# Attention values as 64-row products in two row groups and two banks

## The chip, the cores and the metric

The kernel runs on one core of a Trainium2 chip. The metric is device microseconds of one execution of the whole program, the median of several runs. Three runs of the kernel before gave 2386.85, 2388.28 and 2392.48 us.

## What is computed

One transformer block on 2048 rows of width 576: a modulated layer norm, attention with 32 heads of 18 columns, a residual, a second modulated layer norm, a SiLU feed-forward of width 4608 and a second residual. All arrays are float32.

```python
def _A_ref(x, wqkv, wo):                       # H = 32, Dh = 18
    qkv = (x @ wqkv).reshape(B, S, 3, H, Dh)   # then q, k, v by head
    scores = jnp.einsum("bhqd,bhkd->bhqk", q, k) * (Dh ** -0.5)
    p = _softmax(scores, axis=-1)
    o = jnp.einsum("bhqk,bhkd->bhqd", p, v)
    return o_rows @ wo
def _B_ref(x, w1, w2):
    return _silu(x @ w1) @ w2
h = _layernorm(x) * (1 + ca) + sa
x = x + ga * _A_ref(h, A_wqkv, A_wo)
h = _layernorm(x) * (1 + cb) + sb
x = x + gb * _B_ref(h, B_w1, B_w2)
```

The change touches the einsum that gives `o`, the product of the attention weights and the values.

## The kernel before

The attention runs over four blocks of 512 query rows and, in each block, over eight groups of four heads: 32 groups. A group has 64 score products for its row maxima (`slot_mm`, L896, tile `psa`; VectorE reduces each in L898) and 64 for the weights themselves (`slot_b`, L979, tile `psb`; ScalarE takes the exponential into `pt` in L981). A *slot* is one product of each kind: a `psa` of a later group (38 pairs ahead, `LEAD`) on one half of the array's rows and a `psb` of the present group on the other half, side by side. Everything that contracts over few rows is cut this way, into products of 64 rows whose two halves of the array work at the same time; the code calls this the mode "half".

The values of a group (`pv`, L983) are accumulated over 16 key tiles of 128 rows. For one key tile, four products of 128 rows by 32 columns stand side by side in four column groups, one per head, and write four strips of one bank, `psv` (18 columns of values, one column of ones for the softmax's denominator, padding). One such step of four heads is the unit in which values are scheduled. After the last step ScalarE copies the bank to `ov` (L961), four transposes turn it (`out_b`, L996, `pso`) and VectorE divides by the denominators (L1004, L1007). Products with the full 128 rows and 128 columns, mostly transposes, are a third mode, "full".

Between slots and values TensorE works on *fill*: pieces of the projections in the first block (`psqk`) and afterwards the output projection (`psp`) and the feed-forward (`ps`) of the block before. Fill products are 64-row pairs too (class `Pair`, L652): in the first half of a piece's steps rows 0 to 63 write the first bank and rows 64 to 127 the second, in the second half the other way round, so that each pair of pieces needs two banks at once. ScalarE and VectorE read them out (L1300, L1302, and L1172, L1175 for the residual sums). The last block's own feed-forward has no attention left beside it; it runs at the end in full mode (L646).

The order of TensorE's work is a text, `ORDER`: `s` is a slot, `f` the next piece of fill, a digit that many steps of values, `x` the transposes for maxima or outputs. A class `Sim` reads it and, from a table of durations and a model of the queues, decides where the other engines' instructions are issued; its `rings` say how many banks each use has. The work before the first values is ordered in the same manner by a class `Start`. In total there are 2048 slots and 512 steps of values. The steps stand in 311 unbroken runs of digits.

PSUM has eight banks. Up to the point where the feed-forward begins, `psF` (fill) has two, `psA` (first score products and transposes) three, `psB` (second score products) two and `psV` (values) one. After it, `psF` has three and `psA` two.

Of the kernel before, what the change touches and what calls it, by code (L numbers as in the profile page):

```python
# [73 lines left out]
    "ssffsfsffsfsfssfsfsfsfsfsfsfs11ss1ss1sfsfsfsfsfsfsfssfsfsfssfsfsffss2ss1ss1ss1ss1ssfsfsfssfsfss1ss1xss1ss1sfssfssfssfsfs"  # L74
    "sfsfssfssfss1ssfss1ssfxss11ss1ss1ss1ss1ssfsfssfssfssfssfssfsfss1ss1ss1ss1ss1ss1ss1xss1ssfssfssfssfss11ssfsfssfsfsfssfssf"
    "sxss11ss1ss1ss1ss1ssfsfssfsfsfsfsfs11ssfsfsfsfsfsfssfssfsfsfssfs1ss1ss1xss1ss1ss1ss1ss1ssfsfssfsfs1fssfssfsfsfsxss2ss1ss"
    "1ssfssfsfssfsfsfsfssfssfsfssfsf1ss1ssffss1ss1ss1ss1ss1ss1xss1ssffsfssfssfssfsfsfsfssfssfs1ss1ssffss11fss1ss1ssfssfsxss11"
    "ssffssffss1ss1ss1ssfssfsfsfssfssfssfssfss1ss1ss1xss1ss1ssf1fss1ssfssfsfssfssfsfsxss11ss1ss1sfssfsfsfssfssfssfssfsfss1fss"
    "1ss1ss1ss1ss1ssfssfssfsfssfssfss1xss1ss1ss1ss1ss1sfssfssfssfssfssfssfsxss2ss1ss1ss1ss1ss1ssfss1ssssfsfsfssfssfssfssfssfs"
    "s1ss1ss1xss1ss1ss1ss1ss1ssfssssssfssfsssxss11ss1ss1ss1ssssssfssfssssfss1sssssss1ss1ss1ss1ss1ss1ss1xssssss1ss1ss1sssx1ssf"  # L80
    "ssffss1sff1sfsffsfsfssssf11fssffffsfffssfffffffssffffsffsfs1fffsffffssfffsffffssfffsffffsffsfffffss13fssfsffss1fsfsfsfsf"
    "sfsffssfffsffsffs3xsfsfsfsfsfsffssffsfsfsfsfsfs2sfsfffsfsffssffsfsfsfsfsfs1xsf3ssffssss1ss11fssffsffssffsffssffsfsfs1sfs"
    "fsffssffsfsfs1sfsfsffssffsffss13xsfsfsfsfsfffssffsfsfsfsfsfs12sfsfffssfffssffsfsfsfsffss1sffsx2fss1ss1sss1fssffsffss1fss"
    "fffssfffssf11fsfsffssffsffssffsffssffsff1sffssffsfsffssfffsffsfsfs13xsfsfsfsfsfsfsfssfsfsfsfsfsffss2fssf1fss1ss1xs1fssff"
    "sffss1sfsfsffssffsffss1sfsfsffssffsfsfs12ssffsffssffsfsfs1sffsfsfsfsffssfffssffsfsfs22xsfsfsfsfsfsfsfssfsfsfsfsfsfsfs2fs"
    "sf1ss1ss1ss1ssffsfsfsffsxffffssffsffss1sfsfsffssffsffss2ssffsffssffsffss3sfsfsfsfsfsffssffsfsfsfffss13xsfsfsfsfsfsfsfssf"
    "sfsfsfsffss1ss1ssf1ssffxsf11fssffsffss1sfsfsffssffsfsfs1sfsfsffssffsfsfs2sfsfsffssffsfsfs31ssffsfsfsfsffssfffsfsfsfsfs11"
    "xsfsffsfsfsffss1ss1ss1ssffsfsfsfsfs1ss1ssf11ffffssffffsxffffssffsfsfs1ssffsffssffsffss1sfsfsffssffsffss21sfsfsfsfsfsffss"
    "ffsfsfsfsffss2ss2xfsfsfsfsfsfsfssfsfsfsfsfsfs1ss1ss1sfs111ffffssffsffssffsffssffffsxffffssffffssffsffssffffs2sfffsfsfffs"
    "sffsfsffssffs121fssfffsfsffssffsfsffsfsfs1fsfs1fss1ss1ss1xsfssffsffssffsffssffsfsfs1sfsfsffssffsfsf1fsfsffssffsffss3fsfs"  # L90
    "ffssfffssfffffsffxs12ss1ssfssfs1ssfss1ssfssfs1ss1ssfsfsss1ss1sfsxfssffffssfffsffffssfffffffssffffssffff11fffffffssffffff"
    "fssffffssffffss1ffssfffffssfffffffs112sffffsfffssfffffffssffffsffffsfff1ffx1fsfsfsfsfsffssffsfsfsfsffss111sfsffsfsfsffss"
    "ffsfsfsfsfsfs1sfsffffsffssfffssffsff3xsfsfsffssffsfsfs21sfsfsffssffsffsxffffssffsffss11ssffffssfffsfs2ssffsfsfsfsffssffs"
    "fsfsfsfsfs21ssfffsfsfsffssffsfsfsfsffss22ssffsffssffsffss2xsfsfsffssffsfsfs11sfsfsffssffsffss1fsfsffssffsfsfs111xffsfsff"
    "ffssffsfsfsfsfsfs11ssffffsfsffssffsfsfsfsfsfs211sfsfsffssfffsfs1ssffsffssffsffss2ssffffssffsfsfs11xsfsfsffssffsffss11sfs"
    "fsfsfsfsffssffsffsfsfsfs3xffsfsfsfsffssffsfsfsfsfsfs12ssffffssffsfsfs1ssffsffssffsffss2ssffsffssffffss1sfsfsffssffffss22"
    "xsfsfsfsfsfffssffsfsfsfsffs2sfffsfsfsffssffsfsfsfsfsfs21xffffssffsfsfs1sfsfsffssffsffss11ssffsffssffffss2ssffsffssffsfsf"
    "2ssffsfsfsfsffssffsfsfsfffss112xsfsfsfsfsfsffssfffssffsfsfs2ffffssffsfsfs11ssffsffssffsfsfs11xffffssfffsfs1sfsfsffssffsf"
    "fss1sfsfsffssfffssffsfsfsfsffss22ssffsfsfsfsffssffsfsfsfsffss12xsffsffssffsfsfs21ssffsffssffsffsxffffssffsfsfs1fsfsffssf"
    "fsffss111sfsfsffssfffssffsfsfsfsffss22ssffsfsfsfsffssffsfsfsfsfsfs3sfsfffssffsffssffsffssffsffs2xsfsfsffssffsfsfs1sfsfsf"  # L100
    "fssffsfsfs2sfsfsfsfsfsffssffsffsfffx3ss1fffssf11fssffffssffsfsfs1ssfffffffssfffsfffsfs2sfsfffssfffsfs1sfffsffffssffffsff"
    "fssffffssffffss11xsfsfffsfffssfffsfsffsfs31fsfsffsfffssfffsffsffs1sffffssffffsfffssffx11fsfsfsfsfffssffsfsfsfsfsfs21ssff"
    "fsfsfsffssffsfsfsfsffss3fsfsfsffsffssffsfsfsfsfsfs11sffffssfffssf1xsfsfsffssffsfsfs22sfsfsffssffsffsxffffssffsfsfs21sfsf"
    "sfsfsfsffssffsfsfsfsffss3ssfffsfsfsffssffsfsfsfsfsfs1fsfffssfffsfs1ssffsffssffsffss2ssffffssffffss112xsfsfsffssffsffss2f"
    "ssffsfsfsffssffsfsfsfsfsfs3xffsfsfsfsffssffsfsfsfsfsfs12sffsffssffsfsfs1sfsfsffssffsfsfs1ssffsffssffsffss2sfsfffssfffssf"
    "211xsfsfsfsfsfsffssffsfsfsfsfsfs11sffsfsffsffssfffsfsfsfsfs13xffsffssffsfsfs1sfsfsffssffsffss11ssffsffssffsfsfs11ssffsff"
    "ssffsffss2sfsfsfsffsffssffffssfffss21xsfsffsfsfsffssffsfsfsfsfsfs11sffffssfffssf2xffffssffsffss11fsfsffssffsfsfs1sfsfsff"
    "ssfffsfs2fssffsfsfsffssffsfsfsfsfsfs22sfsfsfsfsfsffssffsfsfsfsfsfs111xsfsfffssffsffss11ssffsffssffsffsxffffssffsfsfs12ss"
    "ffsffssfffssf11sfsfsfsfsfsffssffsfsfsfsfsfs111ssfffsfsfsffssffsffssffsfs111ssffffssffffs1sfsfffssffsfsfs2xsfsfsffssffsff"
    "ss11sfsfsffssffsfsfs11xsfsfsfsfsfffssfffsfsfsfsfs111sfsffssffsffssffsfsfsfsffss111sffsffssffsfsfs1ssffsffssffsfsfs12ssff"  # L110
    "sffssffsfsfs1fssfffssffsffs21ffx"
# [34 lines left out]
class Sim:  # L146


    def __init__(self, fill, ends, loads):
# [6 lines left out]
        self.rings = {"f": [0] * 2, "a": [0] * 3, "b": [0] * 2, "v": [0]}  # L156
# [230 lines left out]
    def values(self, n):  # L387
# [187 lines left out]
def tile_adaln_block(ctx: ExitStack, tc: tile.TileContext, x, wqkv, wo, w1, w2, c, wfirst, wcol, out):  # L575
# [1273 lines left out]
```

## Time and profile before

| what | us |
|---|---|
| median of three runs | 2388.28 |
| profiled execution | 2393.49 |
| its span, first to last instruction | 2391.7 |
| TensorE busy | 2336.2 |
| VectorE busy | 1782.0 |
| ScalarE busy | 1487.1 |
| GpSimd busy | 584.7 |
| first and last start of a value product | 171.1 and 2110.8 |

The span is from the first to the last instruction; the time of the execution has a little around it. In the profile PE is TensorE, PEld its weight loads, DVE VectorE, ACT ScalarE, POOL GpSimd and SP the queue that issues the transfers. Timeline rows give the start, the duration until the last of the merged instructions ends, the engine, the line, and what is written from what. Matmuls overlap and their ends are modelled, so distances between starts say more than durations. A float32 product appears as two records, since it takes two passes; the score and fill products are of a form that takes one. The granted TensorE clock is 0.998 over the span.

### The profile page before, as it was taken

Reading aid. Unit: us, or ns where it says so; the run is one execution under the profiler, and the core shown is the slowest. Engines: PE = TensorE matmul, PEld = TensorE weight load, DVE = VectorE, ACT = ScalarE, POOL = GpSimd, SP = SyncE. Lnnn points to the kernel's source line nnn. Section 1 sums busy time; section 2 is a strip of 40 time slices with the busy share of each in tenths; the row PEclk is TensorE's granted clock in tenths of the full one; section 3 lists DMA queues with packets and bytes.
Section 4 is the critical chain, followed back from the end, with each engine's and each line's share of the span. In section 5 each row is a group of like instructions: output and inputs, shape, how many; then the busy total and the mean of one; then the engine's idle time right before and its main releaser. Section 6 shows DMA issues by size and latency. Waiting matters only on the chain.

```text
span 2391.7 us, 52731 instructions
## 1 busy us (share of the span) xinstructions
PE 2336.2 (98%) x20528; PEld 1635.2 (68%) x20528; DVE 1782.0 (75%) x3179; ACT 1487.1 (62%) x2711; POOL 584.7 (24%) x729
## 2 busy tenths in 40 slices
PE   5999999999999999999999999999999999999999
PEld 4885545545666666676767777777677777688998
DVE  7878888888877887877777877788878878234333
ACT  4237777776766777766577766776767777722121
POOL 4203233314544334443211111111211111110000
PEclk9999999999999999999999999999999999999999
DMA  7758787756555555555555445454545554435663
GB/s 244 254 187 266 252 255 240 260 173 201 200 182 172 173 191 182 171 191 190 172 183 175 149 157 176 166 181 164 186 157 172 186 191 159 138 122 216 209 206 115
DMA packets 210296, 452.29 MB, mean 189 GB/s; under 512 B 22594, under 2 KB 78306, under 8 KB 210050
## 3 DMA queue, kind: packets, MB, share of 16 engines
q1 hardware_dynamic: 210050, 448.93, 56.7%
q8 instruction: 164, 2.69, 0.5%
q14 instruction: 82, 0.67, 0.1%
HBM read 362.51 MB, written 85.80 MB: 187 GB/s over the span
## 4 chain that ended last, share of the span: by engine, by line
PE 88%; DVE 5%; DMA 3%; POOL 2%; issue 2%; ACT 1%; SPq 0%; ACTq 0%; POOLq 0%; DVEq 0%
PE ps L652 27%; PE psv L989 18%; PE psa L896 13%; PE psb L979 10%; PE ps L646 10%; PE psqk L652 4%; DVE mx L898 2%; PE psv L652 1%; PE psp L652 1%; PE pso L996 1%; DMA raw<-in_w 1%; PE psp L646 1%; DMA kt<-kscr 0%; POOL raw L1069 0%; POOL w2t L1075 0%
## 5 line engine op out<-in xcount | busy, mean ns | idle before, releaser
L898 DVE TENSOR_REDUCE mx<-psa 128x1 f32<-128x512 f32 x2048 | 1343.6, 686 | 288.3 <-PE psb L979 149.6
L981 ACT ACTIVATE pt<-psb 128x512 f32<-128x512 f32 x2048 | 1164.0, 597 | 498.3 <-PE psb L979 293.3
L979 PE MATMUL psb<-qt,kt 56*128 56x512 f32 x2048 | 803.2, 426 | 4.6 <-ACT pt L981 2.4
L896 PE MATMUL psa<-kt,qt 54*128 54x512 f32 x2048 | 753.5, 414 | 8.7 <-DVE mx L898 5.2
L896 PEld LDWEIGHTS psa<-kt,qt 54*128 54x128 f32 x2048 | 358.2, 185 | 258.3 <-DVE mx L898 141.3
L989 PE MATMUL psv<-pt,vt 128*32 128x512 f32 x4096 | 505.1, 601 | 0.0
L652 PE MATMUL ps<-w2t,g 64*128 64x288 f32 x4992 | 423.5, 294 | 3.2 <-POOL w2t L1075 1.6
L652 PEld LDWEIGHTS ps<-w2t,g 64*128 64x128 f32 x4992 | 390.1, 185 | 43.1 <-issue 12.7
L979 PEld LDWEIGHTS psb<-qt,kt 56*128 56x128 f32 x2048 | 363.1, 184 | 44.2 <-ACT pt L981 28.8
L652 PE MATMUL ps<-hh,w1t 64*128 64x512 f32 x2160 | 379.0, 393 | 0.1
L1317 POOL TENSOR_TENSOR g<-etmp,g 128x512 fp32r<-128x512 f32 x108 | 137.8, 1296 | 452.2 <-ACT g L1313 406.9
L989 PEld LDWEIGHTS psv<-pt,vt 128*32 128x32 f32 x4096 | 102.4, 109 | 213.0 <-issue 205.6
L652 PEld LDWEIGHTS ps<-hh,w1t 64*128 64x128 f32 x2160 | 216.0, 186 | 40.2 <-issue 4.7
L1179 POOL TENSOR_TENSOR x<-x,gt 128x288 f32<-128x288 f32 x116 | 93.4, 805 | 543.6 <-ACT gt L1175 537.3
L652 PE MATMUL ps<-hl,w1t 64*128 64x512 f32 x864 | 177.9, 391 | 0.0
L1172 DVE TENSOR_TENSOR x<-ps,x 128x288 f32<-128x288 f32 x184 | 83.7, 455 | 116.2 <-PE ps L646 70.7
L646 PE MATMUL ps<-w2t,g 128*128 128x288 f32 x960 | 130.4, 296 | 1.7 <-ACT g L1313 0.9
L646 PEld LDWEIGHTS ps<-w2t,g 128*128 128x128 f32 x960 | 128.6, 188 | 3.3 <-ACT g L1313 1.2
L1306 ACT ACTIVATE eq<-ps 128x512 f32<-128x512 f32 x36 | 21.5, 598 | 146.4 <-PE ps L646 146.4
L646 PE MATMUL ps<-hh,w1t 128*128 128x512 f32 x360 | 106.9, 390 | 0.5 <-DVE hh L626 0.5
L652 PEld LDWEIGHTS ps<-hl,w1t 64*128 64x128 f32 x864 | 88.4, 186 | 13.9
L1025 POOL CAST w1out<-w1raw 128x320 fp32r<-128x320 f32 x72 | 32.4, 450 | 215.0 <-DMA w1raw<-in_w 189.7
(136 smaller groups left out, 2142.2 us busy)
## 6 DMA issues: line engine op xcount, KB each, us to landing
kt<-kscr SPq DMA_DIRECT2D x1024, 108.0 KB
w1t<-w1s SPq DMA_DIRECT2D x144, 640.0 KB
w2t<-w2s SPq DMA_DIRECT2D x108, 576.0 KB
w1s<-w1out SPq DMA_DIRECT2D x72, 320.0 KB
w2s<-w2t SPq DMA_DIRECT2D x36, 576.0 KB
vt<-vscr SPq DMA_DIRECT2D x32, 608.0 KB
qt<-qscr SPq DMA_DIRECT2D x128, 108.0 KB
w1raw<-in_w SPq DMA_DIRECT2D x72, 160.0 KB
```

The lines of the kernel that those rows point to most:

```text
L646: mm(self.ps[late], lhsT=lhsT, rhs=rhs, start=(i == 0), stop=(i == self.n - 1))
L652: done = mm(self.ps[g], lhsT=lhsT[rows], rhs=rhs[rows], start=(s == 0), stop=(s == 2 * self.n - 1))
L896: mm(ps, lhsT=t["q"][64 * j:64 * j + 54, hp, stt * P:(stt + 1) * P], rhs=t["k", kc, hp][64 * j:64 * j + 54, :], start=True, stop=True)
L898: return lambda: nc.vector.tensor_reduce(t["mx"][:, 2 * j + hp, stt, kc:kc + 1], ps, axis=AX.X, op=ALU.max)
L979: mm(ps, lhsT=t["kb", kt // 4, hp][64 * e:64 * e + 56, kt % 4 * P:(kt % 4 + 1) * P], rhs=t["q"][64 * e:64 * e + 56, hp, :], start=True, st ...
L981: return lambda: nc.scalar.activation(t["P"][kt, hp][:, e, :], ps, AF.Exp, scale=SCALE)
L989: mm(t["ps"][32 * h:32 * h + 32, :], lhsT=t["v"][:, c0:c0 + 32], rhs=t["P"][kt, h // 2][:, h % 2, :], start=(kt == 0), stop=(kt == NKT - 1 ...
L996: nc.tensor.transpose(ps[:, s4, :], ov[:, s4 * P:(s4 + 1) * P], ident)
L1025: nc.gpsimd.tensor_copy(d["out"][:, 1], d["raw"])
L1172: nc.vector.tensor_add(c["x1", j][:, hs], ps, c["x1", j][:, hs])
L1179: nc.gpsimd.tensor_add(c["x1", j][:, HH:], c["x1", j][:, HH:], box.pop("gt"))
L1317: (nc.vector if last else nc.gpsimd).tensor_tensor(gt[:, 1, :], d["t"], f(gt[:, 0, :]), op=ALU.subtract)
```

## The change

Each value product of 128 rows is split into two of 64 rows. Rows 0 to 63 of the key tile go to the bank `v0` and rows 64 to 127 to the bank `v1`; each bank has the four heads' strips. After the last step ScalarE copies the first bank into `ov`, and one VectorE addition per group of heads adds the second bank to it (`tensor_add`, 128x512). Values now have two banks, `psF` has two banks throughout, and `psA` two throughout. The planners' rings say the same, and the table of durations stays as it was. The order text is new: 318 runs of digits instead of 311, and 1938 pieces of fill instead of 1952 before the end, where the remaining ones are then issued.

```diff
 ORDER = (
-    "ssffsfsffsfsfssfsfsfsfsfsfsfs11ss1ss1sfsfsfsfsfsfsfssfsfsfssfsfsffss2ss1ss1ss1ss1ssfsfsfssfsfss1ss1xss1ss1sfssfssfssfsfs"
...
+    "ssffsfsfsfsfsfssfsfsfssfsfssfssfss1ss1ssffss1ss1ss1ss1ss1ss1ss1ssfsfsfssfsfssfssfsfssfsfsfsfs2xsfsfsfsfsfsfsfs1ss1ss1ssf"
...
-        self.rings = {"f": [0] * 2, "a": [0] * 3, "b": [0] * 2, "v": [0]}
+        self.rings = {"f": [0] * 2, "a": [0] * 2, "b": [0] * 2, "v": [0]}
...
-        self.rings.update(f=[at[0]] * 3, a=[at[1]] * 2)
+        self.rings.update(f=[at[0]] * 2, a=[at[1]] * 2)
...
         if k0 + n == NKT:
-            self.push((Op(ACT_, 600, self.real and self.real.ov(i), (("p", ("v", i), 0), ("k", ("ov", i)))),), 0, self.t + 200)
+            e = self.real.ov(i) if self.real else (None, None)
+            self.push((Op(ACT_, 600, e[0]), Op(DVE_, 690, e[1], (("p", ("v", i), 0), ("k", ("ov", i))))), 0, self.t + 200)
...
-    psA = ps0.enter_context(tc.tile_pool(name="psA1", bufs=3, space=PSUM))
+    psA = ps0.enter_context(tc.tile_pool(name="psA1", bufs=2, space=PSUM))
...
                 t["ov"] = att.tile([P, QB], F32, name="ov", bufs=1)
-                nc.scalar.activation(t["ov"], t["ps"], AF.Copy)
-
-            return copy
+                nc.scalar.activation(t["ov"], t["ps"][0], AF.Copy)
+
+            return copy, lambda: nc.vector.tensor_add(t["ov"], t["ps"][1], t["ov"])
...
-            t["ps"] = psV.tile([P, QB], F32, tag="v", name="psv2")
+            t["ps"] = [psV.tile([P, QB], F32, tag=f"v{g}", name="psv2") for g in range(2)]
         for kt in range(k0, k0 + n):
             for h in range(4):
                 c0 = kt * VQ + VW * h
-                mm(t["ps"][32 * h:32 * h + 32, :], lhsT=t["v"][:, c0:c0 + 32], rhs=t["P"][kt, h // 2][:, h % 2, :],
-                   start=(kt == 0), stop=(kt == NKT - 1), tile_position=(0, 32 * h))
+                for g in range(2):
+                    rows = slice(64 * g, 64 * g + 64)
+                    mm(t["ps"][g][32 * h:32 * h + 32, :], lhsT=t["v"][rows, c0:c0 + 32], rhs=t["P"][kt, h // 2][rows, h % 2, :],
+                       start=(kt == 0), stop=(kt == NKT - 1), tile_position=(64 * g, 32 * h))
...
-        psF = ctx.enter_context(tc.tile_pool(name="psF2", bufs=3, space=PSUM))
+        psF = ctx.enter_context(tc.tile_pool(name="psF2", bufs=2, space=PSUM))
```

The ring of the `Start` planner for `psA` goes from three to two as well, and its products that borrowed the value bank now take `v0`.

Three places show what stands where. The first is TensorE at one step of values in the first group, between two slots; `pt` are the attention weights of a key tile and two heads, `vt` the values, and the numbers are those of the buffers. Before:

```order
L979 MATMUL psb_2551<-qt_619,kt2_79 128x512
L989 MATMUL psv2_2276<-pt2_2085,vt0_2093 32x512 x2
L989 MATMUL psv2_2276<-pt3_2086,vt0_2093 32x512 x2
L896 MATMUL psa_2565<-kt4_81,qt_1486 128x512
L979 MATMUL psb_2567<-qt_619,kt3_80 128x512
```

After:

```order
L980 MATMUL psb_2395<-qt_619,kt6_83 128x512
L992 MATMUL psv2_2316<-pt4_2087,vt0_2093 32x512
L992 MATMUL psv2_2317<-pt4_2087,vt0_2093 32x512
L992 MATMUL psv2_2316<-pt4_2087,vt0_2093 32x512
L992 MATMUL psv2_2317<-pt4_2087,vt0_2093 32x512
L992 MATMUL psv2_2316<-pt5_2088,vt0_2093 32x512
L992 MATMUL psv2_2317<-pt5_2088,vt0_2093 32x512
L992 MATMUL psv2_2316<-pt5_2088,vt0_2093 32x512
L992 MATMUL psv2_2317<-pt5_2088,vt0_2093 32x512
L897 MATMUL psa_2411<-kt0_77,qt_1450 128x512
```

Four products into one bank are now eight that alternate between two; the four rows of one `pt` are two heads in two halves.

The second is VectorE around the end of the first group's values, where `psa` are first score products and `psqk` a projection. Before, the reciprocal and the first divisions of the transposed output stand between the reductions, and nothing there reads the value bank:

```order
L898 TENSOR_REDUCE mx_2316<-psa_2983 128x1
L898 TENSOR_REDUCE mx_2316<-psa_2987 128x1
L898 TENSOR_REDUCE mx_2316<-psa_3004 128x1
L898 TENSOR_REDUCE mx_2316<-psa_3010 128x1
L1004 RECIPROCAL rec_3040<-pso_3022 128x16
L1007 TENSOR_TENSOR ot_3027<-pso_3022,rec_3040 128x72
L898 TENSOR_REDUCE mx_2316<-psa_3036 128x1
```

After:

```order
L899 TENSOR_REDUCE mx_2300<-psa_3010 128x1
L726 TENSOR_TENSOR qkhl_3030<-psqk_2776,qkhl_3030 128x512
L726 TENSOR_TENSOR qkhl_3033<-psqk_2777,qkhl_3033 128x512
L899 TENSOR_REDUCE mx_2300<-psa_3038 128x1
L964 TENSOR_TENSOR ov_3042<-psv2_2317,ov_3042 128x512
L899 TENSOR_REDUCE mx_2300<-psa_3054 128x1
L899 TENSOR_REDUCE mx_2300<-psa_3069 128x1
```

The addition stands between two reductions.

The third is TensorE between two groups of heads, here the seventh and the eighth: the last value products of the one and what follows. Before, these rows and 32 more come ahead of the next group's first value product:

```order
L989 MATMUL psv2_6552<-pt3_2086,vt0_2093 32x512 x2
L896 MATMUL psa_7018<-kt1_78,qt_6522 128x512
L979 MATMUL psb_7020<-qt_5859,kt3_80 128x512
L896 MATMUL psa_7024<-kt1_78,qt_6522 128x512
L979 MATMUL psb_7026<-qt_5859,kt3_80 128x512
L652 MATMUL psqk_6738<-hTl_107,wqh_6276 128x512
L652 MATMUL psqk_6739<-hTl_107,wqh_6276 128x512
L652 MATMUL psqk_6738<-hTh_106,wqh_6276 128x512
L652 MATMUL psqk_6739<-hTh_106,wqh_6276 128x512
L896 MATMUL psa_7034<-kt4_81,qt_6522 128x512
L979 MATMUL psb_7036<-qt_5859,kt2_79 128x512
L896 MATMUL psa_7040<-kt4_81,qt_6522 128x512
```

After:

```order
L992 MATMUL psv2_6957<-pt3_2086,vt0_2093 32x512
L897 MATMUL psa_7565<-kt4_81,qt_6943 128x512
L980 MATMUL psb_7567<-qt_6197,kt3_80 128x512
L897 MATMUL psa_7585<-kt4_81,qt_6943 128x512
L980 MATMUL psb_7587<-qt_6197,kt3_80 128x512
L897 MATMUL psa_7595<-kt5_82,qt_6943 128x512
L980 MATMUL psb_7597<-qt_6197,kt2_79 128x512
L992 MATMUL psv2_7603<-pt4_2087,vt1_2094 32x512
```

Here 43 rows between the groups became 6. Over the first fifteen groups, nine have 14 rows there after the change and three have 5 to 7; before, they had 7 to 80.

More of the change, by code (lines that the diff above doesn't have):

```diff
@@ new lines @@
+    "sx1sssfssfssfssfsfssfss1ss1ss1ss1ss1fsfssfssfsfsfsfs1fs1xssfsfssfsfssfsfssfssfss1ss1ss1sfss1ss1ss1ss1ss1ssffsx1ssfsfssfs"
+    "fss1fss1ss1sfssfsfsfsfssfsfssfs1ss1ss1ss1xss1fssfsfssfssfssfssfss1fss1ssffs1ss1ss1ss1ssffsx1ssfsfssfssfss1ss1ss1fsfsfssf"
+    "sfssfsfs1fssfsfssfssfss1ss1ss1ss1xss1ss1ssfsfsfssfsfssfsfssfsfssfss1ssffs1ss1ss1ss1ss1ss1sx1sfssfssfssfsfssfssfssfsfss1s"
+    "s1ss1ss1ss1ss1xssfssfssssssssfss1ss1ss1sss1ss1sx1ssssssssssssssss1ss1ss1ss1ss1ss1ssssssssssss1ss1ss1xss1ss1ss1ss1ssx1ssf"
@@ new lines @@
+    "sfssfs1ssff1ssfffffffssffffsfffssfffffffssfffffffss1fssffffffssfffsffffssfffffffssfffffsffs31fssffs1ffssffssffsfsffssffs"
+    "ffssfffss1fffsfsfffssfffsfsfsffs3xsfsfsfsfsfsffssffsfsfsfsfsfs21fsffs1ss1xs1fssffsfsfs1sfsfsffssffsfsfs11sfsfsffssffsffs"
+    "s1sfsfsffssffsffss2sfsfsfsfsfsffssffsfsfsfsffss112xsfsfsfsfsfsffssffsfsfsfsfsfs1fss11sfsfs1xs11sfssfsfsffss1sfsfsffssffs"
+    "ffss1sfsfsffssffsfsfs2sfsfsffssffsfsfs111ssffsfsfsfsffssffsfsfsfsfsfs111xsfsfsfsfsfsfsfssfsfsfsfsfs1ss1ss1ssffs21sfsfffs"
@@ L112 @@
+    "sxffffssfffsfs2fssfffssffsffss11ssffsfsfsfsffssffsfsfsfsffss12ssffsffssfffssffsfsfsfsfsfs121xssffsffssffsfsfs1ssffsffssf"
+    "fsffss1sfsfsffssffsffss3xssffsffssffsfsfs111ssffsfsfsfsffssffsfsfsfsffss21ssffsffsfsffssffsfsfsfsfsfs12fsfsffssffsffssff"
+    "sffssffsfsfs31ffffx"
 )
@@ L1431, in start_tasks @@
     def start_tasks(st):
[L1432 removed]
+        S0 = Start({"b": 2, "f": 2, "v": 1, "a": 2, "xt": XTB, "wm": KT, "et": ETB, "vst": VSB, "qk": QKB, "raw": 2, "wq": 2, "kt": NKB // 2})
         add, dma = S0.add, S0.dma
@@ L1576, in part @@
                 if n == 0:
-                    d["s", key] = (psV if ring == "v" else psF).tile([P, 512], F32, tag=ring, name="ps" + key[0])
+                    d["s", key] = (psV if ring == "v" else psF).tile([P, 512], F32, tag="v0" if ring == "v" else ring, name="ps" + key[0])
                 for i in range(14)[PARTS[n]]:
```

64 lines of the change are left out of this document (26 added, 38 removed).

## The prediction

> **What bounds the kernel now.** I read the page first, for the engine that sets the end.
>
> ```profile
> PE 2336.2 (98%) x20528; PEld 1635.2 (68%) x20528; DVE 1782.0 (75%) x3179; ACT 1487.1 (62%) x2711; POOL 584.7 (24%) x729
> PE 88%; DVE 5%; DMA 3%; POOL 2%; issue 2%; ACT 1%; SPq 0%; ACTq 0%; POOLq 0%; DVEq 0%
> L989 PE MATMUL psv<-pt,vt 128*32 128x512 f32 x4096 | 505.1, 601 | 0.0
> ```
>
> TensorE is busy 98% of the span and carries 88% of the chain that ended last; the value products (L989) are 4096 records, eight for each step of one key tile and four heads (every float32 product counts twice). Then I cut the span into its stages, because shares hide where an engine has room.
>
> ```profile
> core 0: us, PE busy (x) PEld busy (x) DVE busy (x) ACT busy (x) POOL busy (x), PEclk, DMA share, GB/s
> 0.00:171.00 171.00, 139.42 (x1223) 121.41 (x1223) 135.04 (x280) 61.82 (x108) 49.23 (x63) 0.99 0.70 230
> 171.00:561.00 390.00, 386.08 (x2687) 193.54 (x2686) 343.43 (x600) 295.31 (x547) 104.69 (x151) 1.00 0.74 239
> 561.00:1215.00 654.00, 645.08 (x6071) 436.70 (x6073) 527.22 (x929) 449.18 (x819) 272.36 (x354) 1.00 0.56 183
> 1215.00:2112.00 897.00, 894.83 (x8885) 637.58 (x8883) 666.20 (x1157) 628.28 (x1154) 149.66 (x150) 1.00 0.50 167
> ```
>
> Values run from 171 to 2112 us. From 561 on TensorE is alone at the limit (VectorE has 127 us free of 654, then 231 of 897). In the first block, 171 to 561, VectorE is at 343 of 390 too. A microsecond more on TensorE is therefore a microsecond on the clock after 561, and VectorE work costs something only before it. So the question is what a value step and its surroundings cost on TensorE. Busy time can't tell that, since products overlap; the timeline gives starts.
>
> ```profile
> 1006.46 0.61 PE L989 MATMUL psv<-pt,vt 128*32 128x512 f32 x4
> ...
> 1007.34 0.39 PE L896 MATMUL psa<-kt,qt 54*128 54x512 f32 x1
> 1007.66 1.06 PE L989 MATMUL psv<-pt,vt 128*32 128x512 f32 x8
> 1008.65 0.50 PE L896 MATMUL psa<-kt,qt 54*128 54x512 f32 x1
> ...
> 1009.00 0.39 PE L896 MATMUL psa<-kt,qt 54*128 54x512 f32 x1
> ...
> 1011.44 2.78 PE L989 MATMUL psv<-pt,vt 128*32 128x512 f32 x24
> 1014.15 1.98 PE L652 MATMUL ps<-w2t,g 64*128 64x288 f32 x24
> ```
>
> ```profile
> 1345.34 0.39 PE L652 MATMUL ps<-hl,w1t 64*128 64x512 f32 x2
> 1345.57 0.39 PE L652 MATMUL ps<-hh,w1t 64*128 64x512 f32 x2
> ```
>
> A run of one step takes 1007.66 to 1008.65 = 0.99 us until the next 64-row product starts, a run of three steps 1011.44 to 1014.15 = 2.71. The difference of two steps is 1.72, so a step costs 0.86, and each run has 0.99 - 0.86 = 0.13 on top. Pairs of 64-row products follow each other every 0.23 (second fence). Into the run it takes 0.32 instead (1007.34 to 1007.66), 0.09 more; after it the second pair comes 0.35 after the first (1008.65 to 1009.00), 0.12 more. So a run costs 0.09 + 0.13 + 0.12 = 0.34 us for going in and coming out. The order text holds 512 steps in 311 runs of digits: 512 x 0.86 = 440 us of products and 311 x 0.34 = 106 us of changing over. A gain from this change would have to come from those two.
>
> **Part 1, the products themselves.** Four products of 128 rows by 32 columns become eight of 64 by 32: the same part of the array, the same 512 columns, twice each. I see no reason for another step time, and take 0.86 again. What grows is the stagger:
>
> ```profile
> L989 PE MATMUL psv<-pt,vt x2200: 592/592/619, 1006.0 to 2110.8; 128*32 128x512 f32 x184
> ```
>
> Four products that each last 592 ns cover 0.61 us (first row of the timeline above), so each starts about 18/3 = 6 ns after the one before. Eight of them end 7 x 6 = 42 ns after the first instead of 18. Inside a run the tiles keep their own pace; at its end the next mode waits for the last. That is 24 ns for each run. The order after has 318 runs: 318 x 0.024 = **7.6 us**; it is nothing at best, and twice that if the starts also delay the first pass. The Trainium skill's page TensorE: Matmul & The Clock Gate (Part 3, Measured speedup vs the span model) puts about 4 ns per tile where this row has 6; by that figure the term would be an estimated 5 us.
>
> **Part 2, the changeover.** The diff keeps 64-row products on both sides of a run, so the only thing that changes between them is the column width, 128 to 32. Does a change of columns alone cost less than one of rows and columns? The trace has that case, where transposes (128 by 128) stand next to values (128 by 32):
>
> ```profile
> 1168.23 0.40 PE L979 MATMUL psb<-qt,kt 56*128 56x512 f32 x1
> 1168.56 1.85 PE L1221 MATMUL psT<-ident,ot 128*128 128x128 f32 x12
> 1170.34 1.07 PE L989 MATMUL psv<-pt,vt 128*32 128x512 f32 x8
> 1171.33 1.09 PE L1221 MATMUL psT<-ident,ot 128*128 128x128 f32 x8
> 1172.26 0.60 PE L996 MATMUL pso<-ident,ov 128*128 128x128 f32 x4
> 1172.79 1.07 PE L989 MATMUL psv<-pt,vt 128*32 128x512 f32 x8
> 1173.79 0.74 PE L652 MATMUL ps<-hh,w1t 64*128 64x512 f32 x4
> ```
>
> Values to transposes, columns alone: 1170.34 to 1171.33 = 0.99. Values to 64-row products, rows and columns: 1172.79 to 1173.79 = 1.00. Half rows to full rows at equal columns: 1168.23 to 1168.56 = 0.33, against 0.32 into values. Every change of the form costs the same, whichever side of it changes. So the changeover stays at 0.34 per run: no gain. The new order has seven runs more, 7 x 0.34 = **2.4 us**.
>
> **Part 3, the joining addition.** 32 additions of 128x512 from a bank and SBUF; the nearest row is the same form:
>
> ```profile
> L725 DVE TENSOR_TENSOR qkhl<-psqk,qkhl 128x512 fp32r<-128x512 f32 x36 | 23.9, 679 | 2.9 <-ACT qkhl L721 2.8
> L898 DVE TENSOR_REDUCE mx<-psa 128x1 f32<-128x512 f32 x2048 | 1343.6, 686 | 288.3 <-PE psb L979 149.6 <-PE psa L896 120.1 <-PE psqk L652 0.6
> ```
>
> 0.68 us each, 22 us in all on VectorE. From 561 on it lies in VectorE's free time, and nobody waits. In the first block eight additions are 5.4 us where VectorE is 88% busy; queued behind an addition that waits for ScalarE's copy are the reductions of L898, on which the next first score products wait. I take **4 us** of 0 to 5.4.
>
> **Part 4, the value banks come free later.**
>
> ```profile
> 1010.31 0.50 PE L896 MATMUL psa<-kt,qt 54*128 54x512 f32 x1
> ...
> 1010.45 0.60 ACT L961 ACTIVATE ov<-psv 128x512 f32<-128x512 f32 x1
> ```
>
> Now the bank is free 1011.05 - 1010.31 = 0.74 us after the first 64-row product that follows the last value step. Then comes the addition: 0.74 + 0.68 = 1.4, and up to 0.69 more when a reduction is running, 2.1. In the new order nine of the first fifteen groups have only 14 rows of products (seven pairs, 7 x 0.23, and 0.21 for coming out and going in: 1.8 us) before the next group's first values, and three have five to seven rows (about 0.9 us). Nine waits of 0 to 0.3 and three of 0.5 to 1.2: 1.5 to 6 us, and I take **3**.
>
> **Part 5, the banks given up.** Fill pairs need two banks. With three, the next pair needed one of the old pair's two read out, with two both. The copies are nearly equal:
>
> ```profile
> L1302 DVE COPY etmp<-ps 128x512 f32<-128x512 f32 x53 | 36.3, 684 | 21.7 <-PE ps L652 21.7
> L1300 ACT ACTIVATE etmp<-ps 128x512 f32<-128x512 f32 x53 | 31.6, 596 | 7.6 <-PE ps L652 7.6
> ```
>
> The later one is 0.09 us longer plus a place behind one reduction (0.69). Both orders put a median of 2 to 3.8 us of score products and values between two pairs, and that is the cover; where it is thin (about 1 us in a tenth of the gaps, some 20), up to 0.5 us shows. I take **2 us** of 0 to 10. At the start the first score products lose their third bank: 38 pairs whose maxima take 0.69 each, **2 us** of 0 to 8, since 171 us hold 135 of VectorE. Fourteen pieces of fill move to the end of the program; there one product of 128 rows does a pair's work, so I cost that at nothing.
>
> **The sum.** 7.6 + 2.4 + 4 + 3 + 2 + 2 = 21 us. The profiled execution took 2393.49 us (span 2391.7), so 2414.5; it lies 5.2 us above the median of the runs, 2388.28, and in their terms that is **2409 us**. With the stagger, the addition and the lost banks at 0, and part 4 at its low end, it is 2388 + 2.4 + 1.5 = 2392; with all at the high ends (15 + 2.4 + 5.4 + 6 + 10 + 8 = 47) 2435.
>
> **Rivals.** First, faster: the changeover vanishes because the row groups stay. The mechanism would be that the values' weights go into one row group while the 64-row products still run in the other, so that the 0.09 going in and the 0.13 coming out are hidden: 318 x 0.22 = 70 us, 2409 - 70 = 2339 us. It decides as soon as a run's entry falls below about 0.27. The Trainium skill's page TensorE: Matmul & The Clock Gate (Part 3, What overlaps and what doesn't) speaks for it: a weight load overlaps a running product only where the row group differs. Against that rule:
>
> ```profile
> 1011.44 0.16 PEld L989 LDWEIGHTS psv<-pt,vt 128*32 128x32 f32 x8 [0.36 <-ACT ov L961]
> ...
> 1011.89 0.13 PEld L989 LDWEIGHTS psv<-pt,vt 128*32 128x32 f32 x4 [0.30 <-issue]
> ```
>
> The second four loads of the run at 1011.44 stand beside the first four products in the same 128 rows, so rows of today's kernel already overlap; and the transposes show that equal rows do not spare the changeover. Chance 0.12.
>
> Second, slower still: a step now has 16 loads and 16 products, one instruction per 27 ns. The densest long stretch is this:
>
> ```profile
> 1341.00 0.96 PE L652 MATMUL ps<-w2t,g 64*128 64x288 f32 x12
> 1341.80 0.40 PE L979 MATMUL psb<-qt,kt 56*128 56x512 f32 x1
> ```
>
> Twelve products and twelve loads in 0.80 us, 33 ns each. If that were a floor, a step would take 32 x 33 = 1.06 us, 0.20 more, 512 x 0.20 = 102 us: about 2511. But those products are long enough by themselves to explain it. Chance 0.05.
>
> Third, no change: the stagger falls into the wait that a changeover has anyway, and the newly made order takes back part of TensorE's idle 9 us (561 to 1215) and 4 us (171 to 561), which pays for the banks. About 2390 us, chance 0.19, of which 0.03 lies below the limit of no change.
>
> **The numbers.** The forecast has 0.64. About 0.3% (7 us, 2381 to 2395) is what a measurement can tell from no change. Faster: 0.12 + 0.03 = 0.15; same: 0.16; slower: 0.64 + 0.05 = 0.69. The range leaves out the first two rivals (0.17) and little else: from 2381, the low edge of the third, to 2433, near the forecast's high end.
>
> **What would show it.** In the profile after: a one-step run of values until the next 64-row product 1.01 to 1.02 us (0.99 now), a further step 0.86, entry 0.32. If entry and exit are shorter, part 2 was wrong; if a step is not 0.86, part 1. The addition should be a VectorE row of about 0.68 us, x32, and the stretch from 171 us to the eighth group's end longer by some 5 to 10 us, the stretches behind it by 0.02 per run. If the total is below 2381, the reading of the transposes as the same case is refuted.

## The result and the profile after

The changed kernel takes 2427.56 us (median of 4 runs, 2423.91 to 2428.29), the kernel before 2388.41 beside it (4 runs, 2386.85 to 2392.48): ratio 1.0158, interval 1.0141 to 1.0176. It is slower by 39 us; the forecast was slower by 21, in the range 2381 to 2433. The profiled execution took 2427.39 us (span 2425.2). Before's profiled execution lies 5.1 us above this median (2393.49), so trace against trace shows 33.5 us of the 39.

Busy times, the chain that ended last, and the group of the value products, from the page of the changed kernel:

```profile
PE 2360.2 (97%) x24572; PEld 1633.2 (67%) x24572; DVE 1808.9 (75%) x3213; ACT 1497.5 (62%) x2709; POOL 581.1 (24%) x727
PE 85%; DVE 6%; DMA 5%; POOL 1%; issue 1%; SPq 1%; ACT 1%; DVEq 0%; ACTq 0%; POOLq 0%
L992 PE MATMUL psv<-pt,vt 64*32 64x512 f32 x8192 | 518.6, 601 | 0.0
```

TensorE is still the bound. The value products are twice as many at the same length, and their group is 13.5 us busier (518.6 against 505.1). About half of that comes with the new order: whole rows in the same order (an experiment below) are busy for 512.1. The chain has 3 points less of TensorE, and 1 more of VectorE and 2 more of DMA. Next the steps of the values, from the changed kernel's timeline (start, length, count of records; a step is now 16):

```profile
1020.65 0.39 PE L897 MATMUL psa<-kt,qt 54*128 54x512 f32 x1
1020.97 1.95 PE L992 MATMUL psv<-pt,vt 64*32 64x512 f32 x32
1022.85 0.49 PE L897 MATMUL psa<-kt,qt 54*128 54x512 f32 x1
...
1036.58 0.40 PE L897 MATMUL psa<-kt,qt 54*128 54x512 f32 x1
1036.91 1.09 PE L992 MATMUL psv<-pt,vt 64*32 64x512 f32 x16
1037.93 0.50 PE L897 MATMUL psa<-kt,qt 54*128 54x512 f32 x1
1038.26 0.39 PE L897 MATMUL psa<-kt,qt 54*128 54x512 f32 x1
```

One step until the next 64-row product: 1036.91 to 1037.93 = 1.02 us (0.99 before). Two steps: 1020.97 to 1022.85 = 1.88, so a further step is 0.86, as before. Into the run 0.32 and 0.33 (0.32 before), and the second pair 0.33 after the first (1037.93 to 1038.26; 0.35 before). This is the forecast's picture almost to the hundredth: over the whole traces the median run of one step takes 996 ns before and 1020 after. That is 318 x 0.024 = 7.6 us of TensorE's time, against a loss of 39. The values' own rows, before and after (records, shortest, median and longest ns, first and last start, form):

```profile
L989 PE MATMUL psv<-pt,vt x4096: 592/592/1062, 171.1 to 2110.8; 128*32 128x512 f32 x196
```

```profile
L992 PE MATMUL psv<-pt,vt x8192: 586/589/1058, 178.5 to 2138.7; 64*32 64x512 f32 x200
L964 DVE TENSOR_TENSOR ov<-psv,ov x32: 679/681/693, 227.0 to 2140.0; 128x512 f32<-128x512 f32 x32
```

The 32 additions take 0.68 us each, as put. The first value product starts 7.4 us later than before (178.5 against 171.1), the last one 27.9 later, the span ends 33.5 later: 7 us are lost ahead of the first values, 21 between, 6 in the tail. The stages, in the columns shown in the prediction:

```profile
core 0: us, PE busy (x) PEld busy (x) DVE busy (x) ACT busy (x) POOL busy (x), PEclk, DMA share, GB/s
0.00:171.00 171.00, 139.07 (x1183) 119.15 (x1185) 131.37 (x274) 58.13 (x101) 46.27 (x58) 0.96 0.68 223
171.00:561.00 390.00, 377.23 (x3479) 174.79 (x3477) 336.80 (x573) 288.24 (x518) 109.02 (x158) 0.99 0.74 237
561.00:1215.00 654.00, 644.40 (x7274) 427.12 (x7274) 532.08 (x939) 445.52 (x813) 261.59 (x346) 0.99 0.54 177
1215.00:2112.00 897.00, 895.09 (x10584) 641.18 (x10580) 691.08 (x1201) 631.04 (x1154) 148.70 (x148) 1.00 0.51 170
```

In the first block TensorE is less busy than before (377.23 of 390 instead of 386.08), and so is VectorE (336.80 against 343.43): both do less per microsecond. The prediction doesn't speak of one column, the granted TensorE clock (PEclk). It is 0.96 and 0.99 in the first two stages against 0.99 and 1.00 before, and 0.991 over the span in each of the four runs (0.998 in before's trace). It isn't a little lower everywhere: the trace has four stretches of 7 to 14 us at half clock, where before has three of 3.4 us. Two of the four lie near the end of the first block; the first row is what came ahead of them:

```profile
545.00:557.00 12.00, 10.00 (x82) 3.73 (x80) 10.33 (x20) 8.38 (x15) 3.20 (x6) 0.99 0.68 216
557.00:567.00 10.00, 9.78 (x52) 2.96 (x50) 7.01 (x11) 5.98 (x11) 6.71 (x10) 0.50 0.75 238
567.00:577.00 10.00, 9.18 (x98) 3.07 (x90) 7.53 (x12) 6.49 (x12) 4.02 (x7) 1.00 0.70 237
577.00:587.00 10.00, 9.74 (x52) 3.23 (x50) 7.23 (x14) 6.00 (x11) 5.76 (x9) 0.51 0.49 164
```

At half clock 52 records of products start in 10 us, at full clock 98. A rough estimate of what goes through the clock is the span times what is missing from 1: 2425 x 0.009 = 22 us, against 2392 x 0.002 = 5 before, so at most 17 us of the loss. That needn't make the clock a cause by itself: in the first row TensorE stood idle for 2 of the 12 us. That such idling brings the clock down isn't shown, since no run has the one without the other.

A steadier measure of progress is how many maxima VectorE has taken, one for each first score product. The stages of that line alone (its busy time and count, then clock and transfers), before:

```profile
0.00:171.00 171.00, 57.80 (x90) 0.99 0.70 230
171.00:561.00 390.00, 317.25 (x500) 1.00 0.74 239
```

and after:

```profile
0.00:171.00 171.00, 54.00 (x84) 0.96 0.68 223
171.00:561.00 390.00, 306.64 (x470) 0.99 0.74 237
```

By 561 us before has done 590 maxima, after 554. At before's pace in the first block, 390/500 = 0.78 us each, the 36 missing ones are 28 us: nearly the whole loss that the traces show is made before the feed-forward begins. The start of the ninth group's first value product, the first behind that block, says the same: 34 us later than before. The waits of TensorE's weight loads in the first 600 us say on whom (us in total, times, longest), before:

```profile
PEld psa L896 <- DVE mx L898: 75.9, 108, 1.2
```

and after:

```profile
PEld psa L897 <- DVE mx L899: 151.8, 283, 1.6
```

A first score product now stands 283 times before a bank whose maximum hasn't been taken, instead of 108 times. No value product stands in that wait, but `psA` has two banks instead of three; whether that is the cause is for the experiments.

### The profile page after: what moved, and what is told of

Read it like the earlier page. It is cut to its first block, busy times and chain, and to the rows that moved or that the text cites. A ratio compares the mean times of both kernels' runs of the same rounds, so it can differ in the third digit from the quotient of the medians.

```text
span 2425.2 us, 60908 instructions
## 1 busy us (share of the span) xinstructions
PE 2360.2 (97%) x24572; PEld 1633.2 (67%) x24572; DVE 1808.9 (75%) x3213; ACT 1497.5 (62%) x2709; POOL 581.1 (24%) x727
## 4 chain that ended last, share of the span: by engine, by line
PE 85%; DVE 6%; DMA 5%; POOL 1%; issue 1%; SPq 1%; ACT 1%; DVEq 0%; ACTq 0%; POOLq 0%
PE ps L653 27%; PE psv L992 18%; PE psa L897 13%; PE ps L647 10%; PE psb L980 8%; DVE mx L899 4%; PE psqk L653 3%; PE psp L653 2%; PE psv L653 2%; DMA kt<-kscr 1%; DMA raw<-in_w 1%; DMA w1raw<-in_w 1%; PE psv L1583 1%; PE pso L999 1%; DMA w1s<-w1out 1%
## 5 line engine op out<-in xcount | busy, mean ns | idle before, releaser
L897 PE MATMUL psa<-kt,qt 54*128 54x512 f32 x2048 | 789.9, 424 | 19.6 <-DVE mx L899 10.0
L897 PEld LDWEIGHTS psa<-kt,qt 54*128 54x128 f32 x2048 | 366.3, 186 | 324.2 <-DVE mx L899 209.8
L992 PE MATMUL psv<-pt,vt 64*32 64x512 f32 x8192 | 518.6, 601 | 0.0
L980 PEld LDWEIGHTS psb<-qt,kt 56*128 56x128 f32 x2048 | 369.5, 185 | 15.5 <-ACT pt L982 5.7
L653 PE MATMUL ps<-hh,w1t 64*128 64x512 f32 x2120 | 372.6, 394 | 0.2 <-ACT etmp L618 0.2
L992 PEld LDWEIGHTS psv<-pt,vt 64*32 64x32 f32 x8192 | 121.3, 106 | 195.7 <-issue 184.3
L653 PEld LDWEIGHTS ps<-hh,w1t 64*128 64x128 f32 x2120 | 209.1, 186 | 44.7 <-issue 4.2
L647 PE MATMUL ps<-hh,w1t 128*128 128x512 f32 x380 | 112.9, 390 | 0.5 <-DVE hh L627 0.5
```

The lines of the kernel that those rows point to most:

```text
L647: mm(self.ps[late], lhsT=lhsT, rhs=rhs, start=(i == 0), stop=(i == self.n - 1))
L653: done = mm(self.ps[g], lhsT=lhsT[rows], rhs=rhs[rows], start=(s == 0), stop=(s == 2 * self.n - 1))
L897: mm(ps, lhsT=t["q"][64 * j:64 * j + 54, hp, stt * P:(stt + 1) * P], rhs=t["k", kc, hp][64 * j:64 * j + 54, :], start=True, stop=True)
L980: mm(ps, lhsT=t["kb", kt // 4, hp][64 * e:64 * e + 56, kt % 4 * P:(kt % 4 + 1) * P], rhs=t["q"][64 * e:64 * e + 56, hp, :], start=True, st ...
L992: mm(t["ps"][g][32 * h:32 * h + 32, :], lhsT=t["v"][rows, c0:c0 + 32], rhs=t["P"][kt, h // 2][rows, h % 2, :], start=(kt == 0), stop=(kt = ...
```

## The experiments

The theory after the result (A): the loss is the third `psA` bank, which serves the whole first block. Rivals, by the letters of the expectations: the join, that is the addition and the value banks that come free later (B), and the new order of the work (C). The fill bank that was given up is tested without a letter. All differences below are medians against the kernel before in the same set.

| kernel | us | against before | ratio, interval |
|---|---|---|---|
| two first-score banks alone | 2422.69 | +33 | 1.0139, 1.012 to 1.0157 |
| two fill banks alone | 2398.05 | +9 | 1.0035, 1.0024 to 1.0047 |
| changed, but whole rows in one bank | 2422.42 | +33 | 1.0135, 1.0118 to 1.0153 |
| new order alone | 2404.98 | +16 | 1.006, 1.0044 to 1.0076 |
| addition alone | 2403.39 | +14 | 1.0058, 1.0044 to 1.0072 |
| split only after the first block | 2410.35 | +21 | 1.0086, 1.0072 to 1.0101 |
| changed, with the old order | 2451.24 | +62 | 1.0254, 1.0238 to 1.027 |
| changed, without the addition | 2425.17 | +36 | 1.0144, 1.0127 to 1.0161 |
| addition that reads SBUF alone | 2402.09 | +13 | 1.0055, 1.0041 to 1.0069 |
| bank read by VectorE, result unused | 2399.27 | +10 | 1.0046, 1.0033 to 1.0059 |
| plan of the addition, none issued | 2391.56 | +2 | 1.0007, 0.9998 to 1.0015 |

### Two first-score banks alone

```diff
-        self.rings = {"f": [0] * 2, "a": [0] * 3, "b": [0] * 2, "v": [0]}
+        self.rings = {"f": [0] * 2, "a": [0] * 2, "b": [0] * 2, "v": [0]}
...
-    psA = ps0.enter_context(tc.tile_pool(name="psA1", bufs=3, space=PSUM))
+    psA = ps0.enter_context(tc.tile_pool(name="psA1", bufs=2, space=PSUM))
...
-        S0 = Start({"b": 2, "f": 2, "v": 1, "a": 3, ...
+        S0 = Start({"b": 2, "f": 2, "v": 1, "a": 2, ...
```

> The kernel before with two banks instead of three for the first score products and the transposes until the feed-forward opens; values, order and addition as before. The profile after shows the loss until the ninth group of heads begins: +7 us when the first slot starts, +34 us at 595 us, about nothing behind it. Theory A (that third bank is what is missed, not only at the start but through the whole first block): 2388 + 25 to 35 = 2413 to 2423 us, all of it before 600 us. Rival B (the join: the addition and the value banks that come free later): at most 2393. Rival C (the new order of the work): at most 2393.

2422.69 us (2418.99 to 2424.63), 33 more than before. The maxima by stage in this kernel:

```profile
0.00:171.00 171.00, 54.91 (x85) 0.97 0.69 224
171.00:561.00 390.00, 308.79 (x473) 1.00 0.70 227
```

and the wait of its first 600 us:

```profile
PEld psa L896 <- DVE mx L898: 156.9, 295, 1.7
```

558 maxima by 561 us (554 in the changed kernel), 295 waits (283). Same values as before, same fill banks, no addition, and the same hole in the same place: theory A holds in the order of before. The clock is 0.996 over this span, 2417 x 0.004 = 10 us by the estimate above, 5 more than before, so most of these 33 us don't go through it. 32 maxima at 0.78 are 25 us, which is the whole difference of the two traces' spans (2417.2 - 2391.7 = 25.5); behind 561 us nothing more is lost.

### Two fill banks alone

```diff
-        self.rings.update(f=[at[0]] * 3, a=[at[1]] * 2)
+        self.rings.update(f=[at[0]] * 2, a=[at[1]] * 2)
...
-        psF = ctx.enter_context(tc.tile_pool(name="psF2", bufs=3, space=PSUM))
+        psF = ctx.enter_context(tc.tile_pool(name="psF2", bufs=2, space=PSUM))
```

> The kernel before with two fill banks instead of three once the feed-forward is open, nothing else changed. All theories: little, 2388 to 2394 us, since both orders put a median of 2 to 3.8 us of other products between two pairs. Should it be above 2400, the fill bank is a cause that the profile after hides behind its new order.

2398.05 us (2397.36 to 2400.84): more than expected. The prediction had 2 of 0 to 10 for it; it is 9, near the upper bound. The two kept traces are only 4.1 us apart, and one place holds all of that: the transposes of the attention's output (`psT`, L1157), which take fill banks. Before:

```profile
1618.49 1.53 PE L1157 MATMUL psT<-ident,ot 128*128 128x128 f32 x12
...
1628.71 1.06 PE L989 MATMUL psv<-pt,vt 128*32 128x512 f32 x8
```

With two fill banks:

```profile
1616.33 1.09 PE L1157 MATMUL psT<-ident,ot 128*128 128x128 f32 x8
...
1625.28 2.23 PE L652 MATMUL ps<-w2t,g 64*128 64x288 f32 x23 [1.74 <-DVE th L1167]
...
1631.35 1.07 PE L989 MATMUL psv<-pt,vt 128*32 128x512 f32 x8
```

From the first transposes to the same values it takes 15.0 us instead of 10.2: the products of the fill now wait for VectorE (L1167, which reads a `psT` bank), and the clock is at half for 3.4 us behind that.

### The changed kernel with whole rows

The changed kernel's banks and order, with the values as before: 128 rows, one bank, no addition.

```diff
...
-                for g in range(2):
-                    rows = slice(64 * g, 64 * g + 64)
-                    mm(t["ps"][g][32 * h:32 * h + 32, :], lhsT=t["v"][rows, c0:c0 + 32], ...
+                mm(t["ps"][32 * h:32 * h + 32, :], lhsT=t["v"][:, c0:c0 + 32], ...
```

> The changed kernel with its order and its two and two banks, but the values as 128-row products in one bank, without the addition. Theory A: only the stagger (7.6 us) and a little of the addition go, 2412 to 2420 us. Rival B: most of the 39 us go, 2395 to 2402. Rival C: as A.

2422.42 us (2419.83 to 2425.46), 5 us less than the changed kernel and 2 above what theory A expected. Its value products, and the wait of its first 600 us:

```profile
L989 PE MATMUL psv<-pt,vt 128*32 128x512 f32 x4096 | 512.1, 606 | 0.0
```

```profile
PEld psa L896 <- DVE mx L898: 152.1, 279, 1.7
```

All that the change does to the values themselves, its stagger and its addition, is 5 us in this order. 33 of the 39 remain without it. Rival B as the main cause is refuted.

### The new order alone

The kernel before with the changed kernel's order text and nothing else.

> The kernel before with the new order text alone: three banks each, values as 128-row products. Theory A: 2384 to 2394 us, the order itself costs nothing. Rival B: the same. Rival C: 2410 to 2425.

2404.98 us (2402.64 to 2405.72), outside what theory A expected (2384 to 2394) and outside rival C's 2410 to 2425. An order that was made for two first-score banks costs 16 us where there are three. The granted clock can account for that. It is 0.991 to 0.994 in the four runs of this kernel and 0.995 to 1.000 in the nine runs of before beside it. Its span and clock, one of its long stretches at half clock, and a later stretch at full clock:

```profile
core 0: 2403.9 us, clock 0.991
```

```profile
541.00:554.00 13.00, 12.48 (x42) 3.78 (x40) 8.98 (x14) 7.76 (x14) 8.63 (x13) 0.50 0.72 233
575.00:590.00 15.00, 14.37 (x97) 5.69 (x93) 12.21 (x24) 10.22 (x21) 0.40 (x1) 1.00 0.38 130
```

By the estimate above that is 2404 x 0.009 = 22 us, 17 more than before: the clock is enough for the whole loss of this run. Why this order meets the half clock so often isn't shown. So rival C can't be dismissed by this run; that takes the opposite one. Together with the run above it prices the two banks in the new order: 2422.42 - 2404.98 = 17 us for both, where the old order has 33 and 9.

### The changed kernel with the old order

> The changed kernel with the order text of before. By theory A the parts add up: 2389 + 33 (first banks, old order) + 9 (fill bank) + 5 (split and join) = 2436 us, 2431 to 2441, so that the new order is worth 9 us with the changed banks though it costs 16 with the old ones. Rival C (the new order is a cause of the loss): below 2425.

2451.24 us (2447.42 to 2453.28), 62 more than before, 24 more than the changed kernel and 10 above the upper bound of what was expected. The new order is a gain for the changed kernel, not the cause of its loss. The expectation had put 5 for split and join, as measured in the new order. With their price in the old order, which the next run gave, the parts add up: 33 for the first-score bank, 9 for the fill bank, 14 for the addition (next) and 7.6 for the stagger make 64, against 62 measured.

### The addition alone

```diff
-            self.push((Op(ACT_, 600, self.real and self.real.ov(i), (("p", ("v", i), 0), ("k", ("ov", i)))),), 0, self.t + 200)
+            e = self.real.ov(i) if self.real else (None, None)
+            self.push((Op(ACT_, 600, e[0]), Op(DVE_, 690, e[1], (("p", ("v", i), 0), ("k", ("ov", i))))), 0, self.t + 200)
...
-            return copy
+            return copy, lambda: nc.vector.tensor_add(t["ov"], t["ps"], t["ov"])
```

> The kernel before, all banks and its order, with one VectorE addition per group of heads more: it adds the value bank to its own copy, which doubles numerator and denominator alike. Theory A (the first bank is the loss, the join is small): 2389 + 0 to 6 = 2389 to 2395 us. Rival B (the join): 2400 or more.

2403.39 us (2400.49 to 2406.43), in rival B's range and not in theory A's: the join has a price of its own in the old order. It is 14 us for 32 operations of 0.68 (21.8 us of VectorE), though VectorE has hundreds of microseconds free behind the first block. Three more runs, all with TensorE's work in the order of the kernel before, ask why: is it the bank held longer, the result that comes later, the plan that puts other instructions elsewhere, or VectorE's time itself? Their edits are shown against the addition alone.

```diff
-            return copy, lambda: nc.vector.tensor_add(t["ov"], t["ps"], t["ov"])
+            return copy, lambda: nc.vector.tensor_add(t["ov"], t["ov"], t["ov"])
```

> The kernel before with an addition per group that reads SBUF alone (the copied values plus themselves, so that numerator and denominator are doubled): the value bank comes free after the copy as before, VectorE has 32 operations more and the group's result is later by one of them. It asks where the 14 us of the addition alone come from; TensorE's order is that of the kernel before here too. Theory A (the bank is held longer): 2389 to 2394. Theory B (the result is later, or VectorE's queue stands behind the addition): 2397 to 2405. Theory C (the plan puts the other engines' instructions elsewhere): 2395 to 2404.

```diff
-            return copy, lambda: nc.vector.tensor_add(t["ov"], t["ps"], t["ov"])
+            def read():
+                dum = att.tile([P, 1], F32, name="dum", bufs=2)
+                nc.vector.tensor_reduce(dum, t["ps"], axis=AX.X, op=ALU.max)
+
+            return copy, read
```

> The kernel before with a reduction of the value bank into a column that nobody reads, in the addition's place: the bank is held by VectorE as well as by ScalarE's copy, but the result doesn't wait for it, and it doesn't wait for the copy. Theory A (bank held longer): 2396 to 2405. Theory B (result later, or the queue behind the addition): 2388 to 2394. Theory C (plan): 2395 to 2404.

```diff
-            return copy, lambda: nc.vector.tensor_add(t["ov"], t["ps"], t["ov"])
+            return copy, None
```

> The kernel before, planned with 0.69 us of VectorE per group that is then not issued: the same instructions as before, a few of VectorE, ScalarE, GpSimd and SyncE at other places in their queues. Theories A and B: 2388 to 2392. Theory C (plan): 2395 to 2404.

In the order shown, the three took 2402.09 (2401.1 to 2403.0), 2399.27 (2398.64 to 2402.25) and 2391.56 us (2388.16 to 2396.36). With the bank released early it still costs 13; with the result released early it still costs 10; with the plan alone 2, which is within what can be told from nothing. So theories A, B and C of these three expectations fail as the one cause. What the two slow kernels share with the addition is an operation of about 0.7 us in VectorE's queue. The weight loads' wait for maxima over the whole trace shows where it goes. Before, with the addition, with the addition from SBUF, with the unused read, and with the plan alone:

```profile
PEld psa L896 <- DVE mx L898: 141.3, 208, 1.5
```

```profile
PEld psa L897 <- DVE mx L899: 156.8, 245, 1.7
```

```profile
PEld psa L897 <- DVE mx L899: 159.8, 256, 1.8
```

```profile
PEld psa L897 <- DVE mx L899: 155.6, 248, 1.5
```

```profile
PEld psa L897 <- DVE mx L899: 142.3, 209, 1.4
```

All three kernels with a real operation have 14 to 18 us more of that wait, the plan alone 1. The fourth reading, that VectorE's time itself delays the maxima behind it and with them the next first score product, was formed after these runs; the waits fit it, no run was made to refute it.

### The changed kernel without the addition

```diff
-                nc.scalar.activation(t["ov"], t["ps"][0], AF.Copy)
+                nc.scalar.activation(t["ov"], t["ps"][0], AF.Copy, bias=1e-9)
...
-            return copy, lambda: nc.vector.tensor_add(t["ov"], t["ps"][1], t["ov"])
+            return copy, None
```

> The changed kernel without the joining addition, so that the second bank, half of the keys, is left out of the result (the copy adds a tiny constant in place of it). Theory A: the split and join are worth 5 us together, nearly all of it the stagger: 2424 to 2428 us, 0 to 4 below the changed kernel. Rival B: below 2418.

2425.17 us (2423.42 to 2427.68), 2.4 less than the changed kernel and within the expectation. What costs 14 in the old order costs 0 to 4 in the new one. Against whole rows in the same order (2422.42) 3 us are left for the stagger, less than its 7.6 us of TensorE's time, but the ranges of the two runs overlap.

### Split only after the first block

Before's order; three first-score banks and whole-row values until the feed-forward begins, then two fill banks, the split and the addition, with the second value bank taken from there on.

```diff
+            if "psW" in mp:
+                t["ps"].append(mp["psW"].tile([P, QB], F32, tag="v1", name="psv2"))
...
+                G = len(t["ps"])
+                for g in range(G):
+                    rows = slice(64 * g, 64 * g + 128 // G)
...
```

> The order of before; three banks for the first score products and whole value products until the feed-forward opens, and from there the 64-row values in two banks, two fill banks and the addition. Theory A: the first block is that of before; what is left is the missing fill bank (9 us measured by itself) and the stagger in some 190 runs (190 x 0.024 = 4.6 us): 2389 + 14 = 2403 us, 2398 to 2406. If the split costs more than the stagger, 2410 or more; if the 64-row values gain something where TensorE alone is the limit, below 2396.

2410.35 us (2409.2 to 2413.09), 4 above the expected 2398 to 2406 and at the edge of what a costlier split would give. The split isn't costlier: the median run of one step is 1020 ns here too. The expectation had not counted the addition's cost behind the first block. The maxima by stage:

```profile
0.00:171.00 171.00, 58.73 (x92) 1.00 0.71 231
171.00:561.00 390.00, 316.14 (x497) 0.99 0.74 240
```

589 by 561 us, against 590 before: with the third bank kept, the first block loses nothing, and the wait for maxima is nearly that of before. Over the whole trace and in its first 600 us, and then the first 600 us of the addition alone:

```profile
PEld psa L897 <- DVE mx L899: 144.9, 214, 1.5
```

```profile
PEld psa L897 <- DVE mx L899: 73.5, 100, 1.4
```

```profile
PEld psa L897 <- DVE mx L899: 85.6, 132, 1.7
```

Behind 600 us the wait is 71.4 us here, 156.8 - 85.6 = 71.2 with the addition alone and 141.3 - 75.9 = 65.4 before. So the additions behind the first block go with 6 us more of waiting in both kernels, which with 9 for the fill bank and 4.6 for the stagger comes near the 21.

It is the best of the kernels with split values, and still 21 us behind the kernel before. No version beats that one.

## Why the prediction was right, and where it was not

**The sign, the bound and the changeover** were right: slower, with TensorE as the bound and no saving at the changeover. The term that carries most of the loss was not (part 5).

**Part 1, the stagger.** Right in place and size: 24 ns per run were put, and the median run of one step grew from 996 to 1020 ns, one of three steps from 2713 to 2737; a further step stayed at 0.86 us. What these 7.6 us cost in the total was measured only as 3, with ranges that overlap. Twenty-four nanoseconds for four more tiles are 6 ns per tile; the figure of about 4 in the Trainium skill's page TensorE: Matmul & The Clock Gate (Part 3, Measured speedup vs the span model) is low here.

**Part 2, the changeover.** Right: values of 64 rows between 64-row products pay the same entry (0.32 to 0.33) as values of 128 rows did. The first rival, by which the changeover vanishes, is refuted; its own threshold was an entry under 0.27. The Trainium skill's page TensorEngine Tiling (Array Packing), Key Properties, says that a change of the tiling mode drains TensorE. The trace agrees as far as it shows that a change costs time, 0.32 to 0.33 us where the next pair of the same form comes after 0.23, and a change of the columns alone costs as much. The second rival, a floor per instruction of 33 ns, is refuted too: 32 instructions of a step still take 0.86 us, 27 ns each.

**Parts 3 and 4, addition and value bank**, 4 + 3 us: the price of the operation was right (0.681 us), and in the new order the two together are 0 to 4. But the reason given, that from 561 us on the addition lies in VectorE's free time and nobody waits, does not hold in general: in the old order it costs 14, with 14 to 18 us more of waiting for maxima. A mean share of 75% says little on whether a queue is free at the places where it is needed. That the bank comes free later was not the main price either: released early it still cost 13.

**Part 5, the banks given up.** This is the step that failed. It has "At the start the first score products lose their third bank: 38 pairs whose maxima take 0.69 each, 2 us of 0 to 8". The third `psA` bank isn't only there at the start: it serves until the feed-forward begins, 590 maxima by 561 us, in the very stage that the prediction itself had marked as the one where VectorE is near its limit. Taken alone in the old order it costs 33 us, four times the upper bound. The fill bank was put at 2 and costs 9 alone, inside its bound of 0 to 10. In the new order both together cost 17.

**The moved pieces of fill**, costed at nothing: from the last value product to the end the changed kernel takes 5.6 us more than before (33.5 - 27.9). That the work ahead of it is relieved by as much was not measured.

**The clock** is in no term of the sum. By the estimate above up to 17 us of the loss go through stretches at half clock, and all that the new order costs with the old banks can.

**The sum.** With the old order the mis-sized terms give 62. The new order, of which the prediction took only the number of runs and the gaps between groups, takes back 24 (2451.24 to 2427.56) and leaves 39. The error of 18 us is therefore not one number: a bank forgotten for the length of a block, less what an order made for two banks recovers. That the time lies in the range, 6 us below its high end, is in part luck: the 25 us by which the bank exceeds its bound and the 24 us that the order recovers stood in no term, and they nearly cancel.

The third rival, no change, is refuted: the order did pay back, but against 62, not against 21.

**What stays open.** Why the new order meets the half clock more often, and whether TensorE's idle moments are what brings it about; how the 39 us divide, since the price of a bank depends on the order (33 and 9, or 17 for both); and the reading of the addition's 14, for which the waits speak but no run was made that could have refuted it.

## What to carry to other kernels

Price a buffer that is given up by the stage where its reader is nearest to its limit, and for as long as the buffer lives, not where it comes first to mind: here one 128x512 bank was worth 33 us in the order that was made for it, more than all that the change did to the products. When an operation is added to an engine with time to spare, ask which of its queue's results TensorE waits for right behind it. And an order written for one set of buffers is tied to it: the same text cost 16 us with three banks and gained 24 with two. Last, look at the granted clock of each stage before looking for a cause in the products: a mean of 0.99 was made of stretches at one half here.

## What the runs showed of the hardware

A change of the column width alone, between products of the same 64 rows, costs as much as a change of rows and columns: 0.32 to 0.33 us in. The prediction had inferred this from transposes beside values; it is now measured on the case itself. At half clock 52 records of products started in 10 us, at full clock 98; all four runs of the changed kernel had a mean of 0.991. Eight value products of 64 rows and 32 columns in two row groups and two banks take the same 0.86 us per step as four of 128 rows in one: twice the instructions cost nothing but 24 ns at the end of each run.
